# Scores of left-over queries: the second tile's heads swap output rows

## The chip, the cores and the metric

The kernel runs on one core of a Trainium2 chip. The metric is device time in microseconds, the median of several executions. Before the change five executions took 1580.12 to 1582.09 us, with a median of 1580.93 us.

## The reference

Attention in which each query keeps its 32 highest scores, followed by a feed-forward block with a hardswish gate. All arrays are float32 in the kernel; `q`, `k` and `v` have the shape (8, 8, 576, 64), that is batch, heads, positions and head dimension.

```python
scores = scale * np.matmul(q, k.transpose(0, 1, 3, 2))          # scale = 1/8
kth = np.partition(scores, -32, axis=-1)[..., -32:-31]
scores = np.where(scores >= kth, scores, -1e9)
scores = scores - np.max(scores, axis=-1, keepdims=True)
attn = np.exp(scores)
attn = attn / (np.sum(attn, axis=-1, keepdims=True) + 1e-09)
x = (attn @ v).transpose(0, 2, 1, 3).reshape(4608, 512)         # heads side by side
h = x @ w_in                                                    # 512 -> 2048
g = h * np.clip(h + 3.0, 0.0, 6.0) / 6.0
out = g @ w_out                                                 # 2048 -> 512
```

## The kernel before, in words

**Tiles.** The 576 positions of a head are 4 x 128 (`J = 4`, `JP = 512`) and a left-over of 64 (`R = 64`). Two heads make a `Pair`: its `qT` and `kT` hold the head dimension on the partitions, the first head on partitions 0 to 63 and the second on 64 to 127. The left-over keys lie in `kr`, where each head has its own block of columns and zeros in the other head's rows. Two pairs (four heads) make a `Duo`, which handles one tile of queries for `u = 0` and `u = 1`, the duo's first and second pair.

**Kinds of duo.** For a full tile of 128 queries each pair has two score rows per partition, one for each head (`nt = 2`). For the 64 left-over queries (`rest`, line 194) the two heads of a pair share the 128 partitions, 64 queries each, and there is one score row per partition (`nt = 1`). There are 16 such duos, two for each of the 8 batches.

**Steps of a duo.** `scores` (lines 200 to 238) multiplies queries and keys into `big`, a PSUM tile of five banks that exists once, and copies the result into `sc` on ScalarE. `top` (243) finds the 32 highest values of each row on VectorE: four rounds of MAX8 (line 250) and MATCH_REPLACE8 (254). `shift` (259, GpSimd) and `exp` (268, ScalarE) turn the row into weights with their sum in `den`, `inverse` (285, VectorE) takes the reciprocal, `weights` (289, GpSimd) scales the row and splits it into 16-bit halves `e16`, `flip` (309) transposes these by DMA from SP's queue, `join` (314) puts the halves back together as `eT` (ScalarE for `u = 0`, mostly GpSimd for `u = 1`), `values` (326) multiplies with the values into `pv` in PSUM, and `place` (347) copies to `xT`, or to `xr` for left-over queries. In `values` of a left-over duo (line 335) head `hh` takes the columns of `eT` that belong to its 64 queries.

**Scores of left-over queries (lines 211 to 223).** For each pair `u` there are two products of 64 x 64 x 512 (line 215: head dimension x queries x keys), then two of 64 x 64 x 64 with the left-over keys (line 217). The first head uses rows 0 to 63 of the array and writes output partitions 0 to 63; the second head uses rows 64 to 127 and writes partitions 64 to 127. Bank `u` of `big` takes the 512 keys, and the fifth bank (`left`) takes the left-over keys of both pairs side by side. Line 219 copies the first two banks, line 220 the fifth.

**Order of the work.** Every engine runs its instructions in the order in which the program issues them. The loop at the end goes over duos and over 8 slots of each. In a slot come one round of `top`, the parts of earlier duos that the tables `usual`, `behind`, `early` and `soon` put there, and a few pieces of the feed-forward block. `duos[m + 1].scores()` is issued in slot 1 of duo `m`, so scores are ready ahead of their search. The feed-forward block of 128 rows (`feed_forward`: `h` at line 365, gate at 373 to 380, `acc` at 385) is cut into pieces that are queued and handed out by `piece`, at a pace set by how many are left. What is left over at the end runs after the last duo. Loads of the values of the next batch (`load_values`, lines 163 and 167) are issued from SP's queue, the same one that issues the transposes of line 312.

Of the kernel before, what the change touches and what calls it, by code (L numbers as in the profile page):

```python
# [29 lines left out]
def kernel(  # L30
# [9 lines left out]
    nc = tc.nc  # L40
    P = nc.NUM_PARTITIONS
    B, H, S, D = q.shape
    DM, FF = moe_w_in.shape
    J = S // P
    JP = J * P
    R = S - JP
# [41 lines left out]
    def big():  # L88

        return ps_big.tile([P, 5 * 512], F32, tag="big", name="big")  # L90
# [48 lines left out]
    class Pair:  # L139


        def __init__(self, b, hp):
            self.b, self.hp = b, hp
            self.vm, self.vr, self.kr = vms[hp], vrs[hp], krs[b % 2 * NHP + hp]
# [40 lines left out]
    class Duo:  # L185
# [3 lines left out]

        def __init__(self, pairs, qt):
            self.pairs, self.qt, self.early = pairs, qt, False
            self.rest = qt == J
            self.nt = 1 if self.rest else 2
            self.nb = J + 2 if self.rest else 2 * J + 1
            self.m, self.less = [None] * 2, [None] * 2
            self.e16, self.t16, self.eT = [None] * 2, [None] * 2, [None] * 2

        def scores(self, us=(0, 1)):  # L200

            if us[0] == 0:
                self.sc = scpool.tile([P, 2, 2 * (S + R)], F32, tag="sc", name="sc")
                self.den = mpool.tile([P, 2, 2], F32, tag="den", name="den")
            sc, nu = self.sc[:, us[0] : us[-1] + 1, :], len(us)
            ps = big()
            heads = [slice(0, D), slice(D, P)]
            qs = slice(self.qt * P, min(self.qt * P + P, S))
            banks = ps[:, 0 : 4 * 512].rearrange("p (n s) -> p n s", s=512)
            left = ps[:, 4 * 512 :]  # L210
            if self.rest:
                for i, u in enumerate(us):
                    pr = self.pairs[u]
                    for d in heads:
                        nc.tensor.matmul(banks[d, i, :], pr.qT[d, qs], pr.kT[d, :])  # L215
                    for hh, d in enumerate(heads):
                        nc.tensor.matmul(left[d, i * R : (i + 1) * R], pr.qT[d, qs], pr.kr[d, hh, :])
                nc.gpsimd.memset(sc[:, :, S : S + R], 0.0)
                nc.scalar.copy(sc[:, :, 0:JP], banks[:, 0:nu, :])
                nc.scalar.copy(  # L220
                    sc[:, :, JP:S], left[:, 0 : nu * R].rearrange("p (u r) -> p u r", r=R)
                )
                return
            for i, u in enumerate(us):
                pr = self.pairs[u]
                nc.tensor.matmul(  # L226
                    left[:, i * P : (i + 1) * P], pr.qT[:, qs], pr.kr[:].rearrange("p h r -> p (h r)")
                )
            for i, u in enumerate(us):
                pr = self.pairs[u]  # L230
                for hh, d in enumerate(heads):
                    nc.tensor.matmul(banks[:, 2 * i + hh, :], pr.qT[d, qs], pr.kT[d, :])  # L232
            nc.scalar.copy(  # L233
                sc.rearrange("p u (h s) -> p (u h) s", h=2)[:, :, 0:JP], banks[:, 0 : 2 * nu, :]
            )
            nc.scalar.copy(  # L236
                sc[:, :, JP : JP + P], left[:, 0 : nu * P].rearrange("p (u r) -> p u r", r=P)
            )
# [87 lines left out]
        def values(self, dst):  # L326

            w = R if self.rest else P
            pv = ps_w.tile([P, 512], F32, tag="w", name="pv")
            for u in range(2):  # L330
                pr, eT = self.pairs[u], self.eT[u]
                for c in range(J + 1):
                    for hh in range(2):
                        if self.rest:
                            rhs = eT[:, c if c < J else J + hh, hh * R : (hh + 1) * R]
                        else:
                            rhs = eT[:, c if hh == 0 or c == J else J + 1 + c, :]
                        nc.tensor.matmul(  # L338
                            pv[hh * D : (hh + 1) * D, u * w : (u + 1) * w],
                            pr.vm[:, hh, c, :] if c < J else pr.vr[:, hh, :],  # L340
                            rhs,
                            start=(c == 0),
                            stop=(c == J),
                        )
            self.pv = dst, pv[:, 0 : 2 * w].rearrange("p (u q) -> p u q", u=2)
# [70 lines left out]
    per_batch = 2 * J + 2  # L416
    ND = len(duos)
# [4 lines left out]
    left = 0  # L422
# [87 lines left out]
    def pair_at(m, first):  # L510

        b, at = divmod(m, per_batch)
        return pairs[b + 1][at - first] if b + 1 < B and 0 <= at - first < NHP else None
# [18 lines left out]
    usual = dict(  # L532
        shift0=3, exp0=4, inverse0=9, weights0=10, flip0=12, join0=15,
        shift1=7, exp1=8, inverse1=13, weights1=14, flip1=16, join1=19, values=22, place=23,
    )

    behind = dict(usual, values=25, place=26)
    early = dict(
        shift0=3, exp0=3, inverse0=4, weights0=4, flip0=5, join0=8,
        shift1=7, exp1=7, inverse1=8, weights1=8, flip1=9, join1=12, values=12, place=13,  # L540
    )
    soon = dict(
        shift0=3, exp0=3, inverse0=5, weights0=5, flip0=7, join0=10,
        shift1=7, exp1=7, inverse1=9, weights1=9, flip1=11, join1=14, values=16, place=17,
    )
    queued = {}
    for m in range(ND):
        for part, at in (early if m < 2 else soon if m >= ND - 2 else behind if per_batch <= m < ND - 4 else usual).items():
            queued.setdefault(8 * m + at, []).append((m, part))

    def parts(slot, late=None):

        for m, part in sorted(queued.get(slot, []), key=lambda x: x[1][:-1] != "shift"):
            if late is not None and (part[:-1] in ("inverse", "weights")) != late:
                continue
            if part == "values":
                values(m)
            elif part == "place":
                place(m)
            else:  # L560
                getattr(duos[m], part[:-1])(int(part[-1]))

    due = 0.0
    for m in range(ND + 3):
        u = duos[m] if m < ND else None
        for i in range(8):
# [18 lines left out]
            if i == 0:  # L585
                p = pair_at(m, 4)
# [5 lines left out]
            if i == 5:  # L592
                p = pair_at(m, 5)
# [42 lines left out]
```

## Time and profile before

| | before |
|---|---|
| median of five executions | 1580.93 us (1580.12 to 1582.09) |
| profiled execution | 1580.12 us, span 1578.3 us |
| mean granted TensorE clock | 0.964 |
| busy: TensorE / VectorE | 1457.0 us (92%) / 1466.8 us (93%) |
| busy: ScalarE / GpSimd | 1095.8 us (69%) / 1142.8 us (72%) |
| VectorE: MAX8 (line 250) | 1152 instructions of 743 to 747 ns |
| VectorE: MATCH_REPLACE8 (line 254) | 864 instructions of 743 ns |
| line 215, scores of left-over queries | 128 matmuls, 32.8 us busy |
| line 217, the same with left-over keys | 128 matmuls, 9.0 us busy |
| lines 219 and 220, their copies on ScalarE | 16 x 1010 ns and 16 x 275 ns |

The profile is of one execution. Times in it are counted from the start of its span; the device time of that execution is 1.8 us longer than the span. PE is TensorE, PEld its loading of weights, DVE VectorE, ACT ScalarE, POOL GpSimd, and SP the engine whose queue issues the DMAs. A group of instructions is named by line, engine and operation, with the tiles that it writes and reads. A float32 product shows as two MATMUL records. Matmuls overlap, so the sum of their durations is larger than their busy time. "Idle before" is the time for which the engine stood still just before an instruction, with the instruction that ended it. "issue" is time in which an engine waited for nothing that the profile shows.

### The profile page before, as it was taken

Reading aid. Unit: us, or ns where it says so; the run is one execution under the profiler, and the core shown is the slowest. Engines: PE = TensorE matmul, PEld = TensorE weight load, DVE = VectorE, ACT = ScalarE, POOL = GpSimd, SP = SyncE. Lnnn points to the kernel's source line nnn. Section 1 sums busy time; section 2 is a strip of 40 time slices with the busy share of each in tenths; the row PEclk is TensorE's granted clock in tenths of the full one; section 3 lists DMA queues with packets and bytes.
Section 4 is the critical chain, followed back from the end, with each engine's and each line's share of the span. In section 5 each row is a group of like instructions: output and inputs, shape, how many; then the busy total and the mean of one; then the engine's idle time right before and its main releaser. Section 6 shows DMA issues by size and latency. Waiting matters only on the chain.

```text
span 1578.3 us, 28787 instructions
## 1 busy us (share of the span) xinstructions
PE 1457.0 (92%) x10272; PEld 1039.0 (66%) x10272; DVE 1466.8 (93%) x3105; ACT 1095.8 (69%) x1865; POOL 1142.8 (72%) x1264
## 2 busy tenths in 40 slices
PE   5256799979999999998999999999999999999899
PEld 3152666567767777666777777776777767677675
DVE  6999999999999999999999999999999999999700
ACT  6675777777777777777776786777766787777621
POOL 4868687777867777867687777867687777867841
PEclk9568999989999999999999999999999999999999
DMA  8642543444345543545254443446344443533400
GB/s 236 161 179 44 113 83 83 92 91 97 77 89 90 100 83 75 103 85 119 55 108 74 97 89 81 93 92 118 55 96 87 98 88 74 107 61 68 83 22 14
DMA packets 450319, 144.49 MB, mean 92 GB/s; under 512 B 433280, under 2 KB 441472, under 8 KB 450176
## 3 DMA queue, kind: packets, MB, share of 16 engines
q1 hardware_dynamic: 450176, 142.65, 43.6%
q8 instruction: 81, 1.33, 0.3%
q14 instruction: 62, 0.51, 0.1%
HBM read 45.09 MB, written 9.44 MB: 35 GB/s over the span
## 4 chain that ended last, share of the span: by engine, by line
PE 45%; DVE 42%; POOL 4%; issue 3%; ACT 3%; SPq 1%; DMA 1%; POOLq 0%; ACTq 0%; DVEq 0%
DVE m L250 21%; DVE wk L254 18%; PE h L365 17%; PE acc L385 17%; PE pv L338 5%; PE big L232 3%; DVE y L118 1%; POOL e L306 1%; PE big L177 1%; PE big L215 1%; POOL eT L318 1%; POOL sc L297 1%; DVE a L117 1%; ACT sc L278 1%; PE big L226 1%
## 5 line engine op out<-in xcount | busy, mean ns | idle before, releaser
L250 DVE MAX8 m<-wk 128x8 f32<-128x576 f32 x864 | 613.5, 747 | 2.2
L385 PE MATMUL acc<-w_out,g 128*128 128x512 f32 x1152 | 516.9, 600 | 14.2 <-POOL g L380 14.2
L365 PE MATMUL h<-xT,w_in 128*128 128x128 f32 x4096 | 485.2, 279 | 17.3 <-ACT xT L348 17.3
L365 PEld LDWEIGHTS h<-xT,w_in 128*128 128x128 f32 x4096 | 474.8, 195 | 39.4 <-issue 17.4
L254 DVE MATCH_REPLACE8 wk<-m,wk 128x576 f32<-128x576 f32 x576 | 424.0, 743 | 0.0
L385 PEld LDWEIGHTS acc<-w_out,g 128*128 128x128 f32 x1152 | 213.5, 191 | 260.4 <-issue 238.6
L297 POOL TENSOR_SCALAR sc<-sc,den 128x576 f32<-128x576 f32 x288 | 213.1, 750 | 231.0 <-DVE den L287 228.7
L306 POOL COPY e<-sc 128x2304 uint16<-128x2304 uint16 (+1 forms) x192 | 320.0, 1676 | 10.1
L278 ACT ACTIVATE sc<-sc,shift 128x576 f32<-128x576 f32 x288 | 220.4, 769 | 40.8 <-POOL shift L266 38.1
L318 ACT COPY eT<-t 128x2304 uint16<-128x2304 uint16 (+1 forms) x82 | 215.9, 2633 | 38.0 <-DMA t<-e 35.4
L273 ACT ACTIVATE sc<-sc,m 128x576 f32<-128x576 f32 x288 | 210.1, 777 | 46.2 <-DVE m L250 46.2
L338 PE MATMUL pv<-eT,vm 128*64 128x128 f32 (+1 forms) x2560 | 164.1, 273 | 57.7 <-ACT eT L318 45.7
L254 DVE MATCH_REPLACE8 wk<-m,sc 128x576 f32<-128x576 f32 x288 | 211.9, 743 | 0.0
L318 POOL COPY eT<-t 128x2304 uint16<-128x2304 uint16 (+1 forms) x78 | 203.7, 2612 | 6.2 <-DMA t<-e 5.8
L338 PEld LDWEIGHTS pv<-eT,vm 128*64 128x64 f32 x2560 | 135.3, 141 | 109.1 <-ACT eT L318 49.7
L250 DVE MAX8 m<-sc 128x8 f32<-128x576 f32 x288 | 203.4, 743 | 2.4 <-ACT sc L236 2.4
L373 ACT ACTIVATE g<-h,three 128x512 f32<-128x512 f32 x144 | 98.5, 684 | 149.9 <-PE h L365 140.6
L380 POOL TENSOR_TENSOR g<-g,hs 128x512 f32<-128x512 f32 x144 | 184.8, 1283 | 12.2 <-POOL g L379 0.2
L233 ACT COPY sc<-big 128x2048 f32<-128x2048 f32 (+1 forms) x65 | 119.2, 1834 | 25.7 <-PE big L232 25.6
L232 PE MATMUL big<-kq 64*128 64x512 f32 x512 | 136.5, 653 | 0.0
L379 POOL TENSOR_SCALAR g<-g 128x512 f32<-128x512 f32 x144 | 89.0, 618 | 62.6 <-ACT g L373 52.6
L395 ACT ACTIVATE o<-acc 128x512 f32<-128x512 f32 x36 | 21.4, 595 | 107.1 <-PE acc L385 107.1
(47 smaller groups left out, 1113.4 us busy)
## 6 DMA issues: line engine op xcount, KB each, us to landing
landed<-in_k_dram SPq DMA_DIRECT2D x64, 128.0 KB, 2.8
landed<-in_q_dram SPq DMA_DIRECT2D x64, 128.0 KB, 2.9
st<-in_moe_w_in_dram SPq DMA_DIRECT2D x16, 512.0 KB, 5.0
vm<-in_v_dram SPq DMA_DIRECT2D x64, 128.0 KB, 2.3
st<-in_moe_w_out_dram SPq DMA_DIRECT2D x16, 512.0 KB, 6.2
out_dram<-o SPq DMA_DIRECT2D x32, 256.0 KB, 2.4
t<-e SPq DMA_TRANSPOSE x160, 4.6
landed<-in_k_dram SPq DMA_DIRECT2D x32, 32.0 KB, 2.5
```

The lines of the kernel that those rows point to most:

```text
L232: nc.tensor.matmul(banks[:, 2 * i + hh, :], pr.qT[d, qs], pr.kT[d, :])
L250: nc.vector.max(self.m[u][:, t, 8 * r : 8 * r + 8], self.cur[t])
L254: nc.vector.match_replace(wk, self.m[u][:, t, 8 * r : 8 * r + 8], self.cur[t], LOWEST)
L273: nc.scalar.activation(row, row, AF.Prelu, bias=m[:, t, TOP_K - 1 : TOP_K], scale=-1.0, alpha=FLAT)
L278: nc.scalar.activation(row, row, AF.Exp, bias=self.less[u][:, t : t + 1], scale=-scale / FLAT, accum_out=self.den[:, u, t : t + 1],)
L297: nc.gpsimd.tensor_scalar(row, row, self.den[:, u, t : t + 1], 1.0, ALU.mult, ALU.mult)
L306: nc.gpsimd.tensor_copy(halves[:, :, to : to + c1 - c0], words)
L318: copy(eT[:, 0 : self.nb, :] .rearrange("p c q -> p (c q)") .bitcast(U16) .rearrange("p (x h) -> p h x", h=2), self.t16[u][:, 0 : 2 * self ...
L338: nc.tensor.matmul(pv[hh * D : (hh + 1) * D, u * w : (u + 1) * w], pr.vm[:, hh, c, :] if c < J else pr.vr[:, hh, :], rhs, start=(c == 0), ...
L365: nc.tensor.matmul(h[:, (f - f0) * P : (f - f0 + 1) * P], w_in[:, i, f * P : (f + 1) * P], xT[:, i, :], start=(i == 0), stop=(i == NHP - 1),)
L380: nc.gpsimd.tensor_tensor(g[:], g[:], hs[:], ALU.mult)
L385: nc.tensor.matmul(acc[:], gs[f // nf][:, f % nf * P : (f % nf + 1) * P], w_out[:, f, :], start=(f == 0), stop=(f == NFC - 1),)
```

## The change

The two heads of the second pair (`u = 1`) swap output partitions: its first head now writes partitions 64 to 127, and its second head 0 to 63. So the four products of a left-over duo are each in a quarter of the array of their own (rows of the array from the head, columns from the output partitions). All four products with the 512 keys are issued first, then all four with the left-over keys. These last no longer go to the fifth bank but to the first 64 columns of banks 2 and 3, one bank for each pair, and line 220's copy reads them from there. In `values`, head `hh` of pair `u` finds its 64 queries in block `u ^ hh` of `eT`'s columns. The choice of the slot table is written as `if`/`elif`/`else` in place of one expression, with the same outcome.

```diff
@@ Duo.scores
             if self.rest:
-                for i, u in enumerate(us):
-                    pr = self.pairs[u]
-                    for d in heads:
-                        nc.tensor.matmul(banks[d, i, :], pr.qT[d, qs], pr.kT[d, :])
-                    for hh, d in enumerate(heads):
-                        nc.tensor.matmul(left[d, i * R : (i + 1) * R], pr.qT[d, qs], pr.kr[d, hh, :])
+                quarters = [
+                    (i, hh, d, heads[u ^ hh])
+                    for i, u in enumerate(us)
+                    for hh, d in enumerate(heads)
+                ]
+                for i, hh, d, to in quarters:
+                    pr = self.pairs[us[i]]
+                    nc.tensor.matmul(banks[to, i, :], pr.qT[d, qs], pr.kT[d, :])
+                for i, hh, d, to in quarters:
+                    pr = self.pairs[us[i]]
+                    nc.tensor.matmul(banks[to, 2 + i, 0:R], pr.qT[d, qs], pr.kr[d, hh, :])
                 nc.gpsimd.memset(sc[:, :, S : S + R], 0.0)
                 nc.scalar.copy(sc[:, :, 0:JP], banks[:, 0:nu, :])
-                nc.scalar.copy(
-                    sc[:, :, JP:S], left[:, 0 : nu * R].rearrange("p (u r) -> p u r", r=R)
-                )
+                nc.scalar.copy(sc[:, :, JP:S], banks[:, 2 : 2 + nu, 0:R])
                 return
@@ Duo.values
                         if self.rest:
-                            rhs = eT[:, c if c < J else J + hh, hh * R : (hh + 1) * R]
+                            rhs = eT[:, c if c < J else J + hh, (u ^ hh) * R :][:, 0:R]
@@ choice of the slot table
     for m in range(ND):
-        for part, at in (early if m < 2 else soon if m >= ND - 2 else behind if per_batch <= m < ND - 4 else usual).items():
+        if m < 2:
+            when = early
+        elif m >= ND - 2:
+            when = soon
+        else:
+            when = behind if per_batch <= m < ND - 4 else usual
+        for part, at in when.items():
             queued.setdefault(8 * m + at, []).append((m, part))
```

## The prediction

> **What bounds the kernel now.** I read the page first, for the busy shares. Then I cut the span into stages, listed the waits of VectorE (DVE), and followed the chain of waits and the timeline around each of those waits. The page's first line of engine totals:
>
> ```profile
> PE 1457.0 (92%) x10272; PEld 1039.0 (66%) x10272; DVE 1466.8 (93%) x3105; ACT 1095.8 (69%) x1865; POOL 1142.8 (72%) x1264
> ```
>
> TensorE and VectorE are nearly level, so the average does not say which one decides. The stages do (each row: the stretch, its length, then busy time and instruction count of PE, PEld, DVE, ACT and POOL, then granted clock and DMA):
>
> ```profile
> 205.00:732.90 527.90, 508.85 (x3662) 359.11 (x3660) 524.54 (x1125) 388.83 (x665) 392.58 (x442) 0.98 0.46 91
> 732.90:1369.70 636.80, 633.40 (x4608) 456.06 (x4610) 633.95 (x1359) 464.09 (x794) 482.69 (x535) 1.00 0.45 89
> 1369.70:1495.50 125.80, 121.14 (x918) 89.26 (x914) 119.12 (x259) 89.14 (x149) 95.65 (x101) 1.00 0.39 74
> 1495.50:1578.30 82.80, 79.02 (x444) 54.92 (x444) 0.17 (x1) 18.46 (x31) 27.31 (x28) 0.97 0.07 17
> ```
>
> From 205 us (where the first scores of left-over queries run) to 1491 us VectorE hardly stops. After that only TensorE works, for 79 us, on feed-forward pieces that were put behind the last attention output. What VectorE waits for in the whole run:
>
> ```profile
> DVE a L117 <- POOL a L109: 13.2, 2, 9.9
> DVE den L287 <- ACT den L283: 9.2, 4, 6.7
> DVE m L250 <- ACT sc L236: 2.4, 2, 1.7
> ```
>
> The 13.2 us and 1.7 of the 2.4 lie before 137 us, ahead of everything that is edited. 6.7 of the 9.2 is the last reciprocal at 1497.8, after all the searching. What is left behind 205 us are three stalls, 0.78 us at 419 and these two:
>
> ```profile
> 1371.14 0.17 DVE L287 RECIPROCAL den<-den 128x1 f32<-128x1 f32 x1 [1.41 <-ACT den L283]
> ...
> 1374.30 0.76 DVE L250 MAX8 m<-sc 128x8 f32<-128x576 f32 x1 [0.68 <-ACT sc L236]
> ```
>
> 0.78 + 1.41 + 0.68 = 2.87 us is all that VectorE could gain between 205 and 1491. Its other gaps there are 0.02 to 0.12 us, between instructions that follow each other anyway.
>
> The chain of waits tells how TensorE gets into this. It runs along VectorE up to 726 us, then over TensorE from 732.9 to 1343.8 with one excursion (ScalarE, 1080.7 to 1089.3), and comes back to VectorE at 1374. The last step back goes over SP's queue (SPq: issues of DMAs):
>
> ```profile
> 1357.28 0.33 SPq L163 DMA_DIRECT2D vm<-in_v_dram  x1
> ...
> 1361.29 0.47 SPq L167 DMA_DIRECT2D vr<-in_v_dram  x1
> 1361.86 2.76 SPq L312 DMA_TRANSPOSE t<-e  x1
> ```
>
> The loads of the next values wait until `pv` (L338, from 1356.16) has read the old ones. The eight loads take SP from 1357.28 to 1361.86, and the transposes of L312 queue behind them, although the first one's input was ready at 1356.68 (the POOL copy at 1354.58 takes 2.10). The eT copy on ScalarE at 1366.50 waits for that transpose, the exponentials and `den` are queued behind the copy, and VectorE stands. So a late TensorE costs 2.09 us here. The stall at 419 has the same shape (`pv` at 401.59, transpose at 408.75, eT copy at 414.11).
>
> **The edited part.** One burst of left-over scores in the timeline of TensorE:
>
> ```profile
> 205.63 1.08 PE L215 MATMUL big<-kq 64*64 64x512 f32 x4
> 206.54 0.28 PE L217 MATMUL big<-kr,kq 64*64 64x64 f32 x4
> 206.66 1.03 PE L215 MATMUL big<-kq 64*64 64x512 f32 x4
> 207.52 0.28 PE L217 MATMUL big<-kr,kq 64*64 64x64 f32 x4
> 207.73 0.70 PE L385 MATMUL acc<-w_out,g 128*128 128x512 f32 x1
> ```
>
> Each product is two MATMULs (64 calls of L215, 128 records). The first four start at 205.630, 205.637, 206.110 and 206.117: the two heads share the array, and the two passes of each follow 0.43 to 0.48 us apart. The pair u=1 begins only at 206.653, after the small products of u=0. From 206.653 to the end of the last small one's turn (207.57 + 0.06) the second half costs 0.98 us. The whole burst, 205.63 to 207.73, costs 2.10.
>
> **Removed:** with u=1 in the two free quarters, its passes run beside those of u=0 and the 0.98 us goes; the burst becomes 2.10 - 0.98 = 1.12 us. There are 16 bursts (128 / 8), so TensorE is relieved of 16 x 0.98 = 15.6 us. No row has four quarters at once, so I bound it. The best case is the 1.12. For halves there are two rows. L232 puts two products in different rows of the array and the same output partitions: eight records in 1.92 us, that is 4 x 0.43 and a start. L338 lets two products read the same rows into different columns: 40 records of 0.11 in 2.33 us, that is 20 turns. Both kinds of sharing are what the four quarters combine, so I take 1.12. If only one waiting product may be overtaken, the second pair's first passes start with the first pair's second ones: three turns of 0.43, 0.11 for the small ones and 0.15 to the next instruction, 1.55 us, a relief of 0.55 a burst. The far end, without any overlap, is a rival below.
>
> At this place a rule speaks against the change. By the trace, the first pass of the second head starts 7 ns after that of the first head, ahead of the first head's second pass, though L215 issues the heads one after the other. "TensorE: Matmul & The Clock Gate" of the Trainium skill, Part 3, says that matmuls start and end strictly in program order. By that rule eight passes written product by product would take at least five turns, 2.15 us by the 0.43 us turn, and the change would bring nothing; the rows disagree with it for two products, and no run here shows four.
>
> **Edits with one answer.** L217's products are the same 128 records and lie in the same turn. L219 keeps its form. L220 reads 2 x 64 from two banks in place of 128 in one: from 0.27 us now to 2 x 0.21 (L183's copy of 64) at most, so 0 to +0.15 us a burst; I take 0, as L219 already reads over two banks at 1010 ns for 2 x 512. ScalarE is idle for 3.67 us before the eT copy at 1366.50, which hides it; were that gone, the one burst at 1354 could cost 0.15. `values` takes other columns of eT in the same shape. The rewritten choice of slot tables issues nothing. No wait is added: nothing is queued anew behind anything, and no DMA moves in SP's order.
>
> **What of it reaches the end.** Every queue keeps its order, so an earlier TensorE only lets others start earlier. At 419: the bursts at 381.79 and 399.49 bring `pv` at 401.59 forward by up to 1.96 us (its eT was ready 2.87 us before it started), so the transpose comes forward by as much, and the 0.78 goes. At 1371 and 1374: to lose both stalls after VectorE is already 0.78 early, `pv` at 1356.16 must be 2.87 us earlier. Bursts at 1335.56 and 1354.06 give 1.96. Before them TensorE may have run into its inputs: the `pv` at 1266.64 started only 0.11 us after its eT, which then comes 0.78 earlier, so about 0.89 of lead survives there. 1.96 + 0.89 = 2.85: both stalls go but for 0.02. After that VectorE has nothing left to gain, and the other 12 us of relief turn into TensorE idle time. What is late next is VectorE's own work up to 1491.
>
> The end is fixed to it: reciprocal at 1486.85, POOL's copies, eT at 1492.78, `pv` at 1495.52, then 79 us of TensorE without a gap:
>
> ```profile
> 1495.52 2.32 PE pv L338 x20
> 1497.84 4.37 PE h L365 x32
> ...
> 1512.51 2.33 PE pv L338 x40
> ```
>
> 20 matmuls take the time of 40, and 32 of `h` take 4.37 where others take 3.57: TensorE restarts at half clock after its 4.41 us of waiting, at a price of 1.16 + 0.80 = 1.96 us. With more lead the wait becomes longer, some 7 us. I take the same price, between 0 and twice it. "TensorE: Matmul & The Clock Gate", Part 1, says that the clock is judged in free-running windows of about 3.4 us, by which the restart would cost between nothing and two windows at half speed, 3.4 us.
>
> **Sum.** The profiled execution took 1580.12 us, 1578.3 of it span. 1580.12 - 2.85 = 1577.3. That execution was the fastest of the five (1580.12 to 1582.09, median 1580.93); against the median the forecast is 1580.93 - 2.85 = 1578.1 us, 0.18% less. A measurement of this kernel tells about 0.2% (3.2 us) from no change, so the forecast itself lies just inside "same".
>
> **Rivals.**
> - No further overlap: hardware lets two products run and the others wait. The burst stays at 2.10 and the time at 1580.9. For it: no row has four. Against it: the two kinds of sharing both exist. Chance 0.10.
> - Slower: the crossed quarters don't share, and each product has the array for itself. Four products of 2 x 0.43, four small ones of 0.11 and 0.15 make 4.03 us, 1.93 more a burst. Eight bursts (799 to 1354) lie on the chain between 732.9 and 1369.7 where VectorE already waits for TensorE, so 15.4 us are added: 1596. It begins to lose as soon as a burst is over 2.10 us, and passes 0.2% at 3.16 / 8 = 0.40 more, 2.50 us. Against it: L232 and L338. Chance 0.07.
> - Slower by clock: longer waits bring more half-clock restarts. One costs up to 1.96, and only those in the last 79 us count in full. From the second one on the gain is gone; for over 0.2% three are needed beyond today's one. Chance 0.03.
> - The whole relief arrives: 1580.9 - 15.6 = 1565.3. It would need VectorE's own work to shrink, which nothing here does. Chance 0.06, for any larger gain whose way I don't see.
>
> **How the numbers follow.** The forecast (a relief of 0.55 to 0.98 a burst, stalls gone or nearly) has 0.74. With 0.55 the lead at 1356 is 0.89 + 1.10 = 1.99 and the gain about 2.0, so 1578.9. Medians of a few runs wander by some 0.6 us and the restart by up to 2, so about a third of it (0.26) falls beyond 3.2 us of gain. Faster 0.26 + 0.06 = 0.32; same 0.48 + 0.10 = 0.58; slower 0.10. The range goes from 1576.7 (full gain, half a restart and good luck in the runs) to 1581.2 (no gain, with the runs' wander); outside lie the two large rivals, the clock and a little of the rest.
>
> **What would show it.** Right: eight records of L215 starting within some 0.05 us for the first four, bursts of about 1.12 us, L215's busy time near 17 us (16 x 1.08) in place of 32.8, TensorE's total near 1441, no stall over 0.3 us on VectorE between 205 and 1491, VectorE's last MAX8 about 2.9 us earlier, and the last `pv` group some 79 us before the end as now. Wrong: bursts over 2.1 us, a stall left at 1370, VectorE's instructions themselves shorter or longer than 743 to 747 ns, or a last stretch that is not 79 us.

## The result and the profile after

The changed kernel takes 1577.45 us (median of 25 executions, 1576.93 to 1578.52), the kernel before 1580.9 us (45 executions, 1579.4 to 1583.7). The ratio is 0.9979, with a 95% interval of 0.9974 to 0.9984: 2.5 to 4.1 us less. The profiled execution took 1577.14 us with a span of 1575.4 us; the profiled one of before took 1580.12 us. In what follows the line numbers of after are those of before plus 6 to 8: the large products of left-over scores are L222 (L215 before), the small ones L225 (L217), MAX8 is L256, the reciprocal L293.

The page's engine totals and its chain by engine, in the changed kernel:

```profile
PE 1448.7 (92%) x10272; PEld 1035.5 (66%) x10272; DVE 1466.7 (93%) x3105; ACT 1097.8 (70%) x1865; POOL 1142.6 (73%) x1264
...
DVE 65%; PE 24%; issue 3%; POOL 3%; ACT 3%; SPq 1%; DMA 0%; POOLq 0%; ACTq 0%
```

VectorE's busy time is the same to 0.1 us. What changed is the chain of work that ended last: before, 45% of it lay on TensorE and 42% on VectorE. One burst (all the left-over scores of one duo) in TensorE's timeline:

```profile
204.57 1.09 PE L222 MATMUL big<-kq 64*64 64x512 f32 x8
205.48 0.29 PE L225 MATMUL big<-kr,kq 64*64 64x64 f32 x8
205.70 2.84 PE L391 MATMUL acc<-w_out,g 128*128 128x512 f32 x6
```

All eight passes (MATMUL records, two for each product) of the large products lie in 1.09 us, where before four took 1.08. The single records start at 0, 7, 14 and 20 ns for the four first passes and at 480 to 500 ns for the second ones. From the burst's start to the next instruction it takes 1.13 us in all 16 bursts, against 2.10. What VectorE waits for in the whole run (total, times, longest):

```profile
DVE a L117 <- POOL a L109: 13.2, 2, 9.9
DVE den L293 <- ACT den L289: 7.2, 2, 6.7
DVE m L256 <- ACT sc L242: 1.5, 1, 1.5
```

Of these, 13.2, 1.5 and 0.44 us lie before 137 us and 6.7 is the last reciprocal. Between 205 and 1488 us VectorE has one gap over 0.1 us, of 0.12. The three stalls of 0.78, 1.41 and 0.68 us are gone. On SP's queue, at the place of the stall at 1371:

```profile
1349.88 2.69 SPq L318 DMA_TRANSPOSE t<-e  x1
1352.67 0.53 SPq L163 DMA_DIRECT2D vm<-in_v_dram  x1
...
1356.88 0.47 SPq L167 DMA_DIRECT2D vr<-in_v_dram  x1
1357.44 2.71 SPq L318 DMA_TRANSPOSE t<-e  x1
```

The transpose behind the eight loads goes at 1357.44, 4.4 us earlier than before, because `pv` starts at 1350.12 in place of 1356.16 and no longer decides when the loads go. The end, in the chain of waits:

```profile
1492.55 1.81 PE pv L344 x20
1494.36 4.87 PE h L371 x32
1499.23 10.30 PE acc L391 x24
```

From this `pv` to the end of the span it is 82.8 us, as before. So the whole gain lies ahead of it, in VectorE's line: the three stalls were 2.87 us, and the profiled executions differ by 2.98 us.

### The profile page after: what moved, and what is told of

Read it like the earlier page. It is cut to its first block, busy times and chain, and to the rows that moved or that the text cites. A ratio compares the mean times of both kernels' runs of the same rounds, so it can differ in the third digit from the quotient of the medians.

```text
span 1575.4 us, 28787 instructions
## 1 busy us (share of the span) xinstructions
PE 1448.7 (92%) x10272; PEld 1035.5 (66%) x10272; DVE 1466.7 (93%) x3105; ACT 1097.8 (70%) x1865; POOL 1142.6 (73%) x1264
## 4 chain that ended last, share of the span: by engine, by line
DVE 65%; PE 24%; issue 3%; POOL 3%; ACT 3%; SPq 1%; DMA 0%; POOLq 0%; ACTq 0%
DVE m L256 33%; DVE wk L260 29%; PE h L371 10%; PE acc L391 8%; PE pv L344 2%; PE big L238 2%; DVE y L118 1%; DVE a L117 1%; ACT sc L284 1%; PE big L177 1%; POOL e L312 1%; POOL eT L324 1%; POOL g L386 1%; DVE den L293 1%; POOL sc L303 1%
## 5 line engine op out<-in xcount | busy, mean ns | idle before, releaser
L256 DVE MAX8 m<-wk 128x8 f32<-128x576 f32 x864 | 613.4, 747 | 2.2
L256 DVE MAX8 m<-sc 128x8 f32<-128x576 f32 x288 | 203.4, 743 | 1.5 <-ACT sc L242 1.5
L381 ACT COPY hs<-h 128x512 f32<-128x512 f32 x144 | 83.4, 579 | 0.0
```

The source lines that it names most:

```text
L256: nc.vector.max(self.m[u][:, t, 8 * r : 8 * r + 8], self.cur[t])
```

## Experiments

Theory A is that of the prediction: four quarters run at once, VectorE's line is the limit, and TensorE's time matters only through a few stalls (gaps in which VectorE stands still). Its rivals: the new order or the bank that is no longer used does it (B), the whole of TensorE's time counts (C), or none of it (D). Each ratio is against executions of the kernel before on the same chip; the three groups of runs ran on three chips. Medians of before were 1581.57 us beside the first four, 1581.46 beside the next four and 1581.39 beside the last.

**Order and banks without the swap.**

```diff
-                    (i, hh, d, heads[u ^ hh])
+                    (i, hh, d, heads[hh])
...
-                            rhs = eT[:, c if c < J else J + hh, (u ^ hh) * R :][:, 0:R]
+                            rhs = eT[:, c if c < J else J + hh, hh * R :][:, 0:R]
```

> All of the change but the swap: four large products first, then four small ones, small results in banks 2 and 3, every head in its old quarter. Theory A (what counts is that four products share the array): two products wait for each quarter, so the burst stays at about 2.1 us, VectorE keeps stalls of about 2.9 us in sum behind 205 us, and the time is that of before, 1580.9 us. Theory B (what counts is the order, or the fifth bank of big that is no longer used): bursts may stay at 2.1 us and the stalls go all the same, 1577.5 us.

1580.69 us, ratio 0.9997 (0.9988 to 1.0006): no change. Burst 2.10 us in all 16. TensorE's timeline of one burst, and VectorE's waits from 200 to 1491 us:

```profile
204.53 1.93 PE L222 MATMUL big<-kq 64*64 64x512 f32 x8
206.29 0.40 PE L225 MATMUL big<-kr,kq 64*64 64x64 f32 x8
```
```profile
DVE den L293 <- ACT den L289: 3.3, 4, 1.4
DVE m L256 <- ACT sc L242: 0.7, 1, 0.7
```

Eight records that need 1.93 us with two quarters in use need 1.09 us with four. The stalls stay, five of them, 4.0 us in sum. Theory B falls.

**The swap in the order of before.**

```diff
-                for i, hh, d, to in quarters:
-                    pr = self.pairs[us[i]]
-                    nc.tensor.matmul(banks[to, i, :], pr.qT[d, qs], pr.kT[d, :])
-                for i, hh, d, to in quarters:
-                    pr = self.pairs[us[i]]
-                    nc.tensor.matmul(banks[to, 2 + i, 0:R], pr.qT[d, qs], pr.kr[d, hh, :])
+                for n in range(0, len(quarters), 2):
+                    for i, hh, d, to in quarters[n : n + 2]:
+                        pr = self.pairs[us[i]]
+                        nc.tensor.matmul(banks[to, i, :], pr.qT[d, qs], pr.kT[d, :])
+                    for i, hh, d, to in quarters[n : n + 2]:
+                        pr = self.pairs[us[i]]
+                        nc.tensor.matmul(banks[to, 2 + i, 0:R], pr.qT[d, qs], pr.kr[d, hh, :])
```

> The swap with the order of before: two large and two small products of the first pair, then those of the second. Theory A1 (a product starts as soon as its quarter is free, however many wait before it): the third and fourth large products pass six waiting ones, burst about 1.13 us, time 1577.5 us. Theory A2 (only a few waiting ones can be passed): the second pair starts at the second passes or at the small ones of the first, burst 1.5 to 2.1 us; at 1.55 us still 1577.5 to 1578 us, at 2.1 us 1580.9 us.

1577.68 us, ratio 0.9976 (0.9966 to 0.9986): the full gain. TensorE's timeline:

```profile
205.17 1.10 PE L223 MATMUL big<-kq 64*64 64x512 f32 x8
206.08 0.31 PE L226 MATMUL big<-kr,kq 64*64 64x64 f32 x8
```

The burst takes 1.15 us. The third and fourth large product start 27 and 33 ns after the first. In the kernel's text four small passes stand before them, which start only at 909 ns and later, and so do the second passes of the first two products, at 480 and 487 ns. So they start ahead of six passes that still wait for their quarters. (The profile doesn't list the order of issue; it is taken from the text.) Issuing four large ones in a row is worth 0.013 us a burst; the swap does all the rest.

**The changed kernel with TensorE's time of before.**

```diff
-                for i, hh, d, to in quarters:
+                for i, hh, d, to in quarters + quarters:
                     pr = self.pairs[us[i]]
                     nc.tensor.matmul(banks[to, i, :], pr.qT[d, qs], pr.kT[d, :])
```

> The changed kernel with its four large products issued twice (the second time over the first, with the same result), so that placement, order and banks are those of after and TensorE's time nearly that of before. Theory A (the time in the burst decides): burst 1.13 + 2 x 0.43 = 1.99 us, 0.11 us less than before; stalls come back to about 2.9 - 8 x 0.11 = 2.0 us, time about 1580 us. Theory B (order or banks decide): 1577.5 us, no stalls.

1581.0 us, ratio 0.9995 (0.9986 to 1.0004). The burst takes 1.99 us, as worked out. TensorE's timeline of one burst, and VectorE's waits from 200 to 1491 us:

```profile
206.01 1.95 PE L222 MATMUL big<-kq 64*64 64x512 f32 x16
207.78 0.29 PE L225 MATMUL big<-kr,kq 64*64 64x64 f32 x8
```
```profile
DVE den L293 <- ACT den L289: 1.3, 2, 0.7
DVE m L256 <- ACT sc L242: 0.7, 1, 0.7
```

2.0 us of stall, at 420 and 1370 again. With the swap in place and the time given back, the gain is gone: it is the time in the burst that counts.

**The kernel before with its large products twice.**

```diff
-                    for d in heads:
+                    for d in heads + heads:
                         nc.tensor.matmul(banks[d, i, :], pr.qT[d, qs], pr.kT[d, :])
```

> The kernel before with its large products issued twice. Burst 2.10 + 4 x 0.43 = 3.82 us, 1.72 more; TensorE gets 27.5 us more in all. Theory A (before, VectorE already waited for TensorE at the end of the stretch 733 to 1370, with 8 bursts in it; beyond that point every microsecond of a burst counts): 8 x 1.72 = 13.8 us more stall, 1594 to 1596 us. Theory C (all of TensorE's time arrives): 27.5 us more, 1608 us. Theory D (TensorE's time does not matter): 1581 us.

1604.78 us, ratio 1.0147 (1.0131 to 1.0162): 23 us more for 27.5 us of work. VectorE's waits from 200 to 1491 us:

```profile
DVE den L287 <- ACT den L283: 25.8, 10, 4.6
DVE m L250 <- ACT sc L236: 0.7, 1, 0.7
```

This is more than theory A said (13.8). The stalls begin early, 0.97 us at 242 and 4.23 at 420, and of ten in the `den` row eight come at 824 or later. VectorE waits again and again from then on, not only at the end of a stretch. So the kernel before stood at a bend: less work on TensorE brought some 3 us of 15, and this one step the other way cost nearly its full time (23 of 27.5).

**SP's queue alone.** In the kernel before, the loads of the values are issued one slot later, behind the transpose that falls due there.

```diff
-            if i == 3 and u and u.pairs[0].b and 1 <= m % per_batch <= 2:
+            if i == 4 and u and u.pairs[0].b and 1 <= m % per_batch <= 2:
                 for p in duos[m - 1].pairs:
                     p.load_values()
```

> The kernel before, TensorE's work untouched, with the loads of the values (load_values) issued one slot later, so that the transpose that falls due in that slot stands ahead of the eight loads in SP's queue. Theory A (a late pv holds the loads, these hold the transpose, that holds ScalarE's eT copy and den): the transpose at 1361.86 goes at 1356.7 when its input is ready, the stalls at 419 and 1371 shrink or go with bursts still at 2.1 us; 1578 to 1579.5 us. Rival (TensorE holds VectorE by the late scores alone, SP's queue is a bystander): stalls and time of before, 1580.9 us.

1579.22 us, ratio 0.9983 (0.9974 to 0.9992), with TensorE's bursts as before (32.8 us busy for L215). SP's queue at the place of the late transpose:

```profile
1351.97 8.76 SPq L312 DMA_TRANSPOSE t<-e  x2
1360.83 0.53 SPq L163 DMA_DIRECT2D vm<-in_v_dram  x1
```

The transposes are out before the loads, and the stalls at 419 and 1371 are gone from the profile. In their place stand 0.73, 0.79 and 0.50 us at 1181, 1271 and 1476, where ScalarE's `den` comes late again; what makes it late there wasn't followed up. The eleven executions fall in two groups, five at 1576.7 to 1577.1 and six at 1579.2 to 1580.9; the profiled one, 1580.88, is of the second. The first group is as fast as the changed kernel, with no work taken from TensorE; no profile shows its stalls. So the queue is shown as the way in which a late `pv` made the stall at 1371, and it isn't the only way to a stall. For the one at 419 it isn't shown, since that one also stays away with the loads in their old place (below).

**The swap in batches 3 to 6 alone.**

```diff
             self.rest = qt == J
+            self.swap = int(3 <= pairs[0].b <= 6)
...
-                    (i, hh, d, heads[u ^ hh])
+                    (i, hh, d, heads[u * self.swap ^ hh])
...
-                            rhs = eT[:, c if c < J else J + hh, (u ^ hh) * R :][:, 0:R]
+                            rhs = eT[:, c if c < J else J + hh, (u * self.swap ^ hh) * R :][:, 0:R]
```

> The swap in batches 3 to 6 alone: bursts of 1.13 us from 622 to 1246 us, 2.10 us in the other eight, the two at 1335 and 1354 among them. By the step of the prediction (what TensorE gains before 1266 is lost there, since it runs into its inputs): nearly no lead at 1356, gain 0.1 us, 1580.8 us. Rival (the inputs themselves wait for TensorE and come earlier with it, so the lead lasts): six bursts between 733 and 1266 give 5.8 us of lead, both stalls at 1371 go, the one at 419 stays: gain 2.1 us, 1578.8 us.

1579.29 us, ratio 0.9986 (0.9977 to 0.9995), 2.2 us less. Bursts take 1.13 us from 622 to 1246 us and 2.10 elsewhere. VectorE has no stall left at 1371, though the last two bursts before it are the long ones. The second of them:

```profile
1350.62 1.93 PE L221 MATMUL big<-kq 64*64 64x512 f32 x8
1352.39 0.40 PE L224 MATMUL big<-kr,kq 64*64 64x64 f32 x8
```

It starts 3.44 us earlier than in the kernel before (1354.06), as does the burst ahead of it (1332.12 against 1335.56). So TensorE's lead, the time by which it is ahead of its run in the kernel before, lasts over more than 100 us, against the step of the prediction. The stall at 419, which this run was expected to keep, is 0.13 us here, though the bursts before it are as long as before. It was 0.78 and 0.50 us in two profiled executions of the kernel before, 0.34 in the order-only kernel, and it is missing in the kernel before with a late pace (below), whose edit begins long after it. So this stall comes and goes without the swap.

**The room that the change made.** From duo 60 on, the feed-forward pieces are handed out a little faster, so that three more stand ahead of the last duo.

```diff
+            due += (left > 8 and 60 <= m < ND) / 32
             piece(int(due))
```

> The changed kernel with a slightly faster pace for the feed-forward pieces from duo 60 on (1/32 more a slot while over 8 are left), which brings three pieces of about 1.75 us ahead of the last duo. Theory A (after the change TensorE has time to spare that VectorE's line can't use, so work can be moved into it from the last 79 us): up to 5.3 us less, about 1572 us. Rival (there is little real spare time, the pieces make VectorE stall again): 1576 to 1579 us with new stalls.

1575.3 us, ratio 0.9960 (0.9948 to 0.9973). The last stretch is 6.9 us shorter (73.43 in place of 80.34 us from the end of the last reciprocal to that of the span), but a stall of 2.39 us is back at 1369. Bringing the pieces forward later:

```diff
+            due += (left > 8 and 72 <= m < ND) / 16
             piece(int(due))
```

> The same three pieces, brought forward within the last eight duos (1/16 more a slot from duo 72 on). Theory A: TensorE's gaps after 1377 us were 0.63, 2.39 and 2.86 us in the changed kernel, which hold up to 5.3 us of pieces only if they fall at the right places; 1573 to 1576 us. Rival: they arrive where TensorE is full, stalls come back, 1577 us or more.

1570.36 us (1569.92 to 1570.77), ratio 0.9931 (0.9917 to 0.9944), better than expected and the best of all. There is no stall on VectorE between 200 and 1488 us, and the last stretch is 71.36 us, 9.0 shorter; 1.6 of that goes to a longer wait before it. TensorE in the stretches 1377 to 1440 and 1440 to 1492 us, first in the changed kernel, then with the pieces (length, then busy time and count of PE, PEld, DVE, ACT, POOL, clock, DMA):

```profile
1377.00:1440.00 63.00, 62.37 (x419) 42.35 (x419) 63.00 (x137) 44.12 (x73) 43.93 (x52) 1.00 0.34 64
1440.00:1492.00 52.00, 47.30 (x369) 36.78 (x367) 48.01 (x105) 34.56 (x57) 42.76 (x40) 0.97 0.46 86
```
```profile
1377.00:1440.00 63.00, 63.00 (x443) 43.16 (x440) 63.00 (x137) 44.00 (x74) 44.19 (x50) 1.00 0.39 66
1440.00:1492.00 52.00, 50.47 (x402) 39.08 (x400) 48.43 (x106) 36.16 (x62) 45.08 (x44) 1.00 0.42 79
```

Not all of the gain is work that was moved. TensorE's last wait is shorter (2.02 us), and its clock stays full behind it; in the changed kernel it is at half. The start of the last stretch (same columns; the granted clock is the third figure from the end), first in the changed kernel, then with the pieces:

```profile
1492.55:1500.00 7.45, 7.45 (x55) 6.64 (x56) 0.17 (x1) 3.88 (x10) 6.80 (x9) 0.77 0.00 0
```
```profile
1492.50:1500.00 7.50, 7.50 (x35) 3.98 (x36) 0.17 (x1) 4.78 (x7) 6.92 (x9) 1.00 0.20 37
```

From the last `pv` wait to the end it is 75.9 us in place of 82.8. Of these 6.9 us some 1.9 are the restart at half clock (worked out below), which leaves 5.0 for the three pieces, within the 5.3 that were expected of them.

The same pace on the kernel before tells how much of this needed the swap:

> The kernel before with the late pace that brought the changed kernel to 1570.4 us (1/16 more a slot from duo 72 on, three pieces). Theory A (the room for these pieces is what the swap freed on TensorE): TensorE is full before, the pieces make VectorE stall at 1371 and behind, the gain of about 7 us shrinks to 0 to 4 us: 1577 to 1581 us. Rival (the pieces had room anyway, the pace alone makes the gain): 7 us below before, 1574 us, so that swap and pace simply add up.

1575.66 us, ratio 0.9962 (0.9950 to 0.9975), with stalls of 0.99, 0.56, 1.46, 0.69 and 1.67 us on VectorE from 1180 us on. It gains 5.7 us, between the two expectations: the pieces had some room without the swap. But with this pace the swap is worth 1575.66 - 1570.36 = 5.3 us (on two chips, whose medians of before are 0.07 us apart), where without it it was worth 3.45.

Two pieces more on the changed kernel (1/10 in place of 1/16), and the same with the later loads:

> The changed kernel with 1/10 more a slot from duo 72 on: two pieces more than with 1/16. Theory A (some room is left): 3.5 us less, about 1567 us. Rival (TensorE is full after 1377 us with three pieces: 63.0 of 63.0 us busy): each further piece makes VectorE or the end later by as much, 1570 to 1573 us, with stalls on VectorE.

> As the one before, and the loads of the values one slot later. If a late pv through SP's queue is how a full TensorE stops VectorE, the stalls that the two further pieces bring are smaller: 1567 to 1570 us, and less than without the later loads. Rival (no such stalls, or others): the same time as without.

1571.82 us (0.9937, 0.9925 to 0.9950) and 1571.63 us (0.9934, 0.9921 to 0.9948). The room is used up: a stall comes back on VectorE, and so does the half clock, for 3.4 us from 1497 on. VectorE's timeline of the first of the two:

```profile
1476.28 0.17 DVE L293 RECIPROCAL den<-den 128x2 f32<-128x2 f32 x1 [2.22 <-ACT den L289]
```

With the later loads the stall is 2.07 us, so the place of these loads in SP's queue is not what makes it.

**The kernel before once more.**

> The kernel before, unchanged, for a second profiled execution. If the stalls behind 205 us are a fixed 2.87 us, they show again at 419 and 1371. If they vary with where TensorE's half-clock stretches fall (the order-only kernel, whose bursts are those of before, had 4.0 us in its execution), their sum is another one between 2 and 5 us, and the device time goes up and down with it.

1580.07 us, with stalls of 0.50, 1.49 and 0.69 us at 420 and 1370: 2.68 us. Beside it stand 2.87 us in the first profiled execution (1580.12 us) and 4.00 us in that of the order-only kernel, whose bursts are the same (1582.34 us). The sum varies, and the time goes partly with it. Of the 2.22 us by which the order-only execution is longer than the first one, 1.14 are stalls and 0.70 lie in the last stretch (81.03 us behind the last reciprocal, in place of 80.33). There the clock is at half for 6.83 us, twice as long as the 3.41 us of the first execution. The same columns for these stretches, first that execution, then the order-only one:

```profile
1495.64:1499.06 3.42, 3.42 (x26) 3.09 (x27) 0.17 (x1) 3.10 (x8) 3.07 (x5) 0.50 0.00 0
```
```profile
1495.16:1501.99 6.83, 4.93 (x32) 4.60 (x33) 0.17 (x1) 3.16 (x8) 6.36 (x8) 0.50 0.19 35
```

## Why the prediction was right, point by point

- **Four quarters at once.** Predicted 1.12 us a burst, measured 1.13. Four products, two in each half of the rows and two in each half of the columns, take 1.09 us where two took 1.08, as the two rows for halves had suggested.
- **Program order.** "TensorE: Matmul & The Clock Gate" of the Trainium skill, Part 3, has matmuls start strictly in program order. The swap in the order of before shows the opposite: a product that stands behind the small ones in the text starts at 27 ns, they at 909. So the statement ahead of the prediction that every engine runs its instructions in the order of issue doesn't hold for the start of TensorE's matmuls. The cautious bound of 1.55 us a burst wasn't needed.
- **VectorE's line as the limit.** Predicted gain 2.85 us, by three stalls of 2.87. All three went (the one at 419 comes and goes by itself), the profiled executions differ by 2.98 us, and nothing else of VectorE moved. The order-only kernel and the doubled products show that it is the burst's time that does it, and the pace runs that much of the rest of the relief was there but unused.
- **The lead at the stall: the term that was mis-sized.** The prediction gave `pv` at 1356.16 a lead of 2.85 us, of which 0.89 survived from before 1266 because "TensorE may have run into its inputs", which were to come only 0.78 us earlier. Measured: 6.04 us. The input of the `pv` at 1266.64, first before, then after:

```profile
1263.72 2.81 ACT L318 COPY eT<-t 128x2304 uint16<-128x2304 uint16 x1
```
```profile
1259.61 2.81 ACT L324 COPY eT<-t 128x2304 uint16<-128x2304 uint16 x1
```

It comes 4.11 us earlier, and so does this `pv` (1262.53). By the starts of the bursts, TensorE was 0.73 us ahead at 799 us; the eight bursts from there on gave 0.96 each; 0.5 was lost between 888 and 977, and 1.9 between 1065 and 1157, where TensorE's wait for `xT` grew from 3.38 to 5.07 us. 0.73 + 7.7 - 2.4 makes 6.0. The inputs came earlier with TensorE, as the run with batches 3 to 6 shows too. The total wasn't hurt, since the stalls cap it at 2.87. That the cap hid the error is luck: in a case with longer stalls the same step would have cost a wrong time.
- **From 2.85 to 3.45.** The medians differ by more than the profiled executions. The profiled execution of before was among the fast ones, with 2.87 us of stalls; another with bursts of the same length had 4.00 us at 1582.34 us. After the change the stalls are gone, and the spread of the executions is 1.6 us in place of 4.3. That the median execution of before had some 3.5 us of stalls fits this, and is not shown. Nor is a second source excluded: in the profiled executions the last stretch is 80.3 us where the half clock lasts 3.41 us, and 80.9 to 81.6 where it lasts 6.83 (order only, changed with TensorE's time of before, later loads, batches 3 to 6), and which of these the other executions had is not known. The result lies at the edge of the 0.2% that the prediction put between "same" and "faster"; it had counted a third of its own case beyond it.
- **TensorE's total.** Predicted near 1441 us, measured 1448.7. L222 fell as forecast (17.4 us busy, from 32.8), and L225 from 9.0 to 4.7. Of the missing 7.7, 2.8 lie before the first burst, where the two executions differ in clock (0.75 after and 0.77 before, from 60 to 205 us). For the remainder the records from the first burst on, each counted up to the next start, show 2.8 us more in `h`; whether that is half clock or waiting isn't settled. In the same count 14.8 us left the score products of all duos and 9.2 us were added as gaps.
- **The end.** The stretch behind the last reciprocal is 80.3 us in both. The restart at half clock cost 0.6 + 1.3 us (`pv` x20 in 1.81 against 1.16, `h` x32 in 4.87 against 3.57), about the 1.96 assumed. The wait ahead of it, which was to grow to some 7 us, is 2.86 in place of 4.41: part of TensorE's lead was spent in an earlier wait of 2.39 us at 1482, with a stretch at half clock behind it that before had not. The granted clock of both stretches after the change:

```profile
1482.97:1486.39 3.42, 3.42 (x18) 3.38 (x17) 3.42 (x10) 0.51 (x2) 2.20 (x3) 0.50 0.02 5
1493.21:1496.63 3.42, 3.42 (x23) 3.09 (x20) 0.17 (x1) 2.91 (x8) 3.15 (x4) 0.50 0.00 0
```

So a second half-clock stretch, a rival of the prediction, did come, but the last `pv` still waited for its `eT` behind it, and it cost no time.

## What to carry to other kernels

When two engines are both over 90% busy, list what each waits for: here 15 us less on TensorE brought about the 2.87 us that VectorE stood still, whatever the chain of waits said about shares. Such a change is worth more once work is moved into the room that it makes, and the pace of that work has to be set anew. A long wait of TensorE has a price of its own when its clock is at half behind it: 1.9 us here, which the best pace avoided. Look also at which queue carries a delay from one engine to the other, since a transpose behind eight loads made a stall that neither engine's own work explains.

## What the runs showed of the hardware

- Four 64 x 64 float32 products in the four quarters of the array take as long as two in two quarters: 8 passes in 1.09 us (4 in 1.08 before), with 4 first passes started within 20 ns.
- A matmul whose quarter is free starts ahead of ones that stand before it in the kernel's text and whose quarter isn't free: at 27 ns, past four that start at 909 ns or later and two that start at 480 and 487.
- Half-clock stretches of 3.41 us began 0.1 to 1.2 us after waits of TensorE of 2.39, 2.86 and 4.41 us near the end; in other executions the stretch at the end was 6.83 us. After the last waits of 2.36 and 2.02 us, with the two paces for three pieces, the clock stayed full.
- A copy of 2 x 64 columns from two PSUM banks takes ScalarE as long as one of 128 from a single bank: medians of 270 ns against 272.
